# Convolution of batch 1 on 64-by-32 tiles with a shifted copy of x made by GpSimd and SyncE's queue

## The chip, the cores and the metric

The kernel runs on one core of a Trainium2 chip. Times are device microseconds. A time "before" or "after" is the median of its runs; the profile is one execution, taken by the hardware profiler. Engines are named TensorE (PE, with its weight loads PEld), VectorE (DVE), ScalarE (ACT), GpSimd (POOL) and SyncE (SP). The queues of GpSimd and SyncE issue most of the DMA transfers. A line such as L583 is a line of the kernel.

## The reference

For eight batches, x has 4224 rows of 192 features, in 8 heads of 24. A causal convolution with seven taps, whose weights are a softmax over the taps for each head, is followed by a mixer of rank 32 along the sequence and by a two-layer MLP with residual:

```
w    = softmax(weight, taps)                       # 8 heads x 7 taps
y[s] = sum_k w[head, k] * x[s - 6 + k]             # zero before the start
t    = y^T U                                       # 192 x 32, U is 4224 x 32
u    = y + (t V)^T                                 # V is 32 x 4224
out  = u + relu(u W1) W2                           # W1 192 x 768, W2 768 x 192
```

## The kernel before

**Tiles and groups.** A batch is 33 tiles of 128 rows; all 264 tiles form 33 groups of eight. The first MLP layer works on whole groups (`w1`, L554, into relu buffers `rl_sb`, of which there are three), the second on pairs of tiles (`w2`, L583; four pieces of 12 matmuls to a group), with the residual added on VectorE (L592) and the output sent on SyncE's queue (L600). PSUM has eight banks that are handed out in turn.

**The convolution.** x of a batch lies in `x_sb` as blocks of 64 rows: partitions 0 to 63 (r = 0) hold 32 blocks, partitions 64 to 127 (r = 1) the other 34. There are two `x_sb` buffers and one buffer `xb_sb`. Two forms exist:

- `conv` (L357 to L391) multiplies blocks with a banded matrix on 64-by-64 tiles of TensorE, the block itself and the block before it (halo) accumulated: eight matmuls a head.
- `conv32` (L317 to L353) uses 64-by-32 tiles. Each output strip of 32 rows then needs the 64 rows that end with it, so half of the strips read `x_sb` and half read `xb_sb`, a copy of x shifted by 32 rows. There too are eight matmuls a head, without accumulation.

`x_shift` (L277 to L315) makes `xb_sb` in six steps, all GpSimd copies: `same` for blocks 0 to 15 and for blocks 16 to 31 (L293, 128 partitions; with a small copy for the two extra blocks of r = 1, L295), and four `ahead` steps of 32 partitions (L305).

In the kernel before, batch 0 and batch 1 use `conv`, all others `conv32`.

**Start.** x of batch 0 is loaded in pieces (`KP`, `x_piece`): blocks for tiles 0 to 9 of both r, then the rest of r = 1, then the rest of r = 0. TensorE is kept busy by `idle` (L151 to L159) until the banded matrices are made by `band_half` (L234). The low-rank sum of batch 0 is taken in two ways: packed in four column strips for tiles that are ready early (`tt_mm`, 27 tiles), split in a high and a low part (`tt_split`) and added up by a matmul with `R4`; and as 128-wide matmuls on a fourfold copy of U (`tt_late`, 6 tiles). For groups 0 and 1, u is transposed by TensorE (`yT_part`, `hT_part`); for all later groups by a DMA transpose on SyncE's queue (`transp`, L498).

**The order of work.** `SLOTS` is written out by hand. A slot names groups for `w1`, groups for `w2`, and what is done ahead of which `w2` piece: `h3` makes u of group 3 (`h_group`) and issues its transpose, `t1` and `s1` are the packed sum and its adding up for batch 1, `c2:0:3:AAD` is a chunk of `conv32` (batch, first head, heads, engines that empty the banks), `d1` is the whole `conv` of batch 1 (with the transpose of group 3 held until its last matmul), `x2:6` issues all six steps of batch 2's shift, `l2:2` is the third load of x of batch 2, held until the last `w2` piece issued. Other loads of x are held until a given place in `w1` (`LOADS`), and the shift steps that are left are put between them.

**Queues.** Every engine and every queue works in program order. GpSimd issues all loads of x and of the weights and makes the shifted copies; SyncE issues the outputs and transposes.

Of the kernel before, what the change touches and what calls it, by code (L numbers as in the profile page):

```python
# [9 lines left out]
BF16 = mybir.dt.bfloat16  # L10
F32 = mybir.dt.float32
# [3 lines left out]
def kernel(  # L15
# [10 lines left out]
    nc = tc.nc  # L26
    P = nc.NUM_PARTITIONS
    B, S, D = x.shape
# [12 lines left out]
    QB = 32  # L41
# [14 lines left out]
    def bank():  # L56
        return psp.tile([P, 512], F32, name="ps", tag="ps")
# [18 lines left out]
    def x_part(b, r, s0, s1):  # L76

        blk = NB0 * r + s0 - 1
        return nc.gpsimd.dma_start(  # L79
            out=xt[b][HB * r : HB * r + HB, s0:s1, :],  # L80
            in_=x[b, blk * HB : (blk + s1 - s0) * HB, :].rearrange("(j p) d -> p j d", p=HB),
        )

    XP = [(0, 1, 17), (0, 17, NB0 + 1), (1, 0, 18), (1, 18, NB1 + 1)]

    KP = [{0: (0, 10), 1: (0, 10)}, {1: (10, NB1 // 2)}, {0: (10, NB0 // 2)}]

    def x_piece(k):
        for r, (k0, k1) in KP[k].items():
            x_part(0, r, (1 - r if k0 == 0 else 2 * k0 + 1), 2 * k1 + 1)  # L90

    def piece_tiles(k):
        return [NB0 // 2 * r + j for r, ks in KP[k].items() for j in range(*ks)]

    x_tile(0)
    x_piece(0)


    I32 = mybir.dt.int32
# [25 lines left out]
    )  # L125
    nlast = NT * 32 - nfull * P
    nc.gpsimd.dma_start(out=Ur[0:nlast, nfull, :], in_=U4[nfull * P :, :])
    for k in range(1, len(KP)):
        x_piece(k)


# [7 lines left out]
                in_=moe_w_ch1[:, m0:m1].rearrange("(c k) m -> k c m", k=HB),  # L139
            )  # L140

    zz = cst.tile([P, P], F32, name="zz")
    nc.vector.memzero(zz[:])

    rq = cst.tile([P, 2], F32, name="rq")
# [2 lines left out]
            nc.vector.memset(rq[QB * r : QB * r + QB, n : n + 1], v * r)  # L148
    wps = bank()

    def idle(n, w=4):  # L151
        for _ in range(n):
            nc.tensor.matmul(
                out=wps[:, 0 : w * P].rearrange("p (n t) -> p n t", t=P),
                lhsT=zz[:],
                rhs=zz[:].unsqueeze(1).to_broadcast([P, w, P]),
                start=True,
                stop=True,
            )  # L159

    idle(4)

# [112 lines left out]
            )  # L277

    band_half(0)
    idle(1, 2)  # L280
    band_half(1)


# [2 lines left out]
    def x_shift(b):  # L286
# [29 lines left out]
            ahead(1, m, NB1),  # L316
        ]  # L317

    steps = []

    def conv32(b, h0, nh, engs):
# [30 lines left out]
                    pp[part][:, 0 : nk[part] * GS].rearrange("p (k a) -> p k a", a=GS),  # L352
                )  # L353

    def conv(b, h0, nh, rs, engs, ks=((0, NB0 // 2), (0, NB1 // 2)), pp=None):

        if yt[b] is None:  # L357
            yt[b] = ys.tile([P, NT, D], BF16, name="y_sb")
        nk = {r: ks[r][1] - ks[r][0] for r in rs}
        if pp is None:  # L360
            pp = {r: bank() for r in rs}
        w = nh * GS
        for hh in range(nh):
            h = h0 + hh
            for halo in range(2):
                for r in rs:
                    for c in range(2):
                        st = 1 - halo + c + 2 * ks[r][0]
                        last = nc.tensor.matmul(  # L369
                            out=pp[r][HB * c : HB * c + HB, 0 : nk[r] * w].rearrange(  # L370
                                "p (k a) -> p k a", a=w
                            )[:, :, hh * GS : hh * GS + GS],
                            lhsT=bands[h // HQ][
                                HB * r : HB * r + HB, h % HQ, HB * halo : HB * halo + HB
                            ],
                            rhs=xt[b][
                                HB * r : HB * r + HB,
                                st : st + 2 * nk[r] - 1 : 2,
                                h * GS : h * GS + GS,
                            ],  # L380
                            start=(halo == 0),
                            stop=(halo == 1),
                            tile_position=(HB * r, HB * c),
                        )
        for n, r in enumerate(rs):
            j0 = NB0 // 2 * r + ks[r][0]
            evac(
                engs[n % len(engs)],
                yt[b][:, j0 : j0 + nk[r], h0 * GS : h0 * GS + w],
                pp[r][:, 0 : nk[r] * w].rearrange("p (k a) -> p k a", a=w),  # L390
            )  # L391
        return last
# [217 lines left out]
    def x_load(b, q, after):  # L610
        if q == 0:
# [5 lines left out]


    SLOTS = [
        ([0], [], {}),  # L620
        ([1], [0], {0: ["h0"], 1: ["h3", "l2:2"], 2: ["l2:3"]}),
        ([2], [1], {0: ["d1", "h1"], 1: ["t1"], 3: ["s1"], 4: ["h4", "x2:6"]}),
        ([3], [2], {1: ["h5"], 3: ["h6"]}),
        (
            [4, 5],
            [3, 4, 5],
            {
                0: ["h7"],
                2: ["c2:0:3:AAD"],
                3: ["c2:3:3:AAD"],  # L630
                4: ["c2:6:2:A", "x3:4"],
                6: ["t2"],
                8: ["s2"],
                9: ["h8"],
                11: ["h9"],
            },
        ),
    ]
    nh = 10
    for k in range(5, 14):  # L640
        gs = list(range(3 * k - 9, 3 * k - 6))
        hs = [f"h{g}" for g in range(nh, min(nh + 3, NG))] + [None] * 3
        nh = min(nh + 3, NG)
        if k == 5:
            at = {
                2: ["c3:0:3:AAD"],
                3: ["c3:3:3:AAD"],
                4: ["c3:6:2:A", "x4:3"],
                5: [hs[0]],
                6: ["t3"],  # L650
                8: ["s3", hs[1]],
                11: [hs[2]],
            }
        elif k < 10:
            b = k - 2
            at = {
                1: [f"c{b}:0:3:AAD"],
                2: [f"c{b}:3:3:AAD"],
                3: [f"c{b}:6:2:A"] + ([f"x{b + 1}:3"] if b + 1 < B else []),
                5: [f"t{b}", hs[0]],  # L660
                7: [f"s{b}"],
                8: [hs[1]],
                11: [hs[2]],
            }
        else:
            at = {0: [hs[0]], 4: [hs[1]], 8: [hs[2]]}
        SLOTS.append((gs, gs, {p: [w for w in what if w] for p, what in at.items()}))
# [5 lines left out]
        LOADS[b] = [(g, 0), (g, 3), (g + 1, 0), (g + 1, 3)]  # L673


    late = piece_tiles(2)
    U4_sb = cst.tile([P, len(late), 4, R], BF16, name="U4_sb")

    def tt_late(p):

        for n, j in enumerate(late):
            nc.tensor.matmul(
                out=p[:, 0:D],
                lhsT=U4_sb[:, n, :, :].rearrange("p a r -> p (a r)"),
                rhs=yt[0][:, j, :],
                start=False,
                stop=(n + 1 == len(late)),
            )

    for h in range(0, H, 2):  # L690
        conv(0, h, 2, [0, 1], "AA" if h == 0 else "AD", KP[0])
    work = [bank() for _ in range(4)]
    tp = bank()
    u_layout(work)
    x_tile(1)
    x_zero(1, nc.gpsimd)
    x_part(1, *XP[0])
    o = 0
    for r, (k0, k1) in KP[2].items():
        j = NB0 // 2 * r + k0  # L700
        nc.gpsimd.tensor_copy(
            out=U4_sb[:, o : o + k1 - k0, :, :],
            in_=U_sb[:]
            .rearrange("p k j r -> p (k j) r")[:, j : j + k1 - k0, :]
            .unsqueeze(2)
            .to_broadcast([P, k1 - k0, 4, R]),
        )
        o += k1 - k0

    NSL = (NT + 7) // 8 * 2  # L710
    V_sb = cst.tile([P, NSL, P], BF16, name="V_sb")
# [13 lines left out]
    W2_sb = cst.tile([P, MC, D], BF16, name="W2_sb")  # L725
    nc.gpsimd.dma_start(out=W2_sb[:], in_=moe_w_ch2[:].rearrange("(m p) d -> p m d", p=P))

    parts0 = [(0, 0, 2, bank(), "A"), (0, 2, 4, bank(), "D"), (1, 0, 4, bank(), "D")]
    yT_part(0, parts0)
    def conv_piece(k):  # L730
        for n, h in enumerate(range(0, H, 3)):
            for r in KP[k]:
                conv(0, h, min(3, H - h), [r], "AD"[n % 2], KP[k], {r: work[n]})

    conv_piece(1)
    tt_mm(0, piece_tiles(0) + piece_tiles(1), tp)
    tt_split(0, tp)
    conv_piece(2)
    ps0 = work[3]
    for n, part in enumerate(ttb[0]):  # L740
        nc.tensor.matmul(out=ps0[:, 0:D], lhsT=R4[:], rhs=part[:], start=(n == 0), stop=False)
    more = [(2, 0, 2, bank(), "A"), (2, 2, 4, bank(), "A")]
    yT_part(0, more[0:1])
    tt_late(ps0)
    yT_part(0, more[1:])
    parts1 = [(0, 0, 4, bank(), "A")]
    yT_part(1, parts1)
    tt_done(0, ps0)
    hT_part(0, parts0 + more)
    rest = [(c, 0, 4, bank(), "ADA"[c]) for c in (1, 2)]  # L750
    yT_part(1, rest)
    hT_part(1, parts1 + rest)
    band2 = cst.tile([P, H, QB], BF16, name="band2")
    for xp in XP[1:]:
        x_part(1, *xp)
# [8 lines left out]
    def do(what):  # L764
        if what[0] == "c":
            b, h0, n, engs = what[1:].split(":")
            conv32(int(b), int(h0), int(n), engs)
            return
        if what[0] == "d":
            for h in range(H):  # L770
                last = conv(int(what[1:]), h, 1, [0, 1], "AA" if h == 2 else "AD")
            held(transp(3), last)
            return
        if what[0] == "l":
            b, q = (int(v) for v in what[1:].split(":"))
# [8 lines left out]
        n = int(what[1:])  # L784
        if what[0] == "h":
            h_group(n)
            if n > 1 and n != 3:
                transp(n)
        elif what[0] == "t":
            tt_split(n, tt_mm(n, range(NT)))  # L790
        else:
            tt_sum(n)
# [55 lines left out]
```

## Time and profile before

| What | Value |
|---|---|
| median of three runs | 325.29 us (325.09 to 325.36) |
| profiled execution | 325.29 us, of which the span of the core is 323.5 |
| busy share of the span | TensorE 98%, weight loads 69%, VectorE 83%, ScalarE 53%, GpSimd 44% |
| one GpSimd copy to `xb_sb`, 128x3072 | 2.74 us |
| one GpSimd copy to `xb_sb`, 32x3072 | 2.74 us |
| output of 192 KB, median from issue to landing | 2.7 us |
| load of x of 384 or 432 KB, median | 7.3 us |
| DMA transpose, median | 3.9 us |

A page of the profile gives each engine's busy time and groups of instructions. A row of the timeline is: start, length, engine, line, operation, output and input, count, and in brackets the idle time ahead of it with what ended it. A row of the chain is: start, length, engine, tile, line. Busy time of TensorE includes waits inside its pipeline, so what it does with its time is read from the order of its work in the chain.

### The profile page before, as it was taken

What the parts mean: (1) busy time and instruction counts of PE and PEld (TensorE: products, weight loads), DVE (VectorE), ACT (ScalarE), POOL (GpSimd) and SP (SyncE); (2) the same over time, 40 slices, a digit from 0 to 9 for tenths busy, and PEclk for the clock granted to TensorE, in tenths of its full rate; (3) what the DMA queues carried; (4) which work ended last, traced back from release to release, by engine and by line L of the source; (5) the groups of instructions that cost most, each with busy time, mean ns of one, the idle gap of its engine ahead of it and who ended that gap; (6) DMA issues with size and microseconds to landing.
All of it is one profiled execution on the core that took longest, in us unless ns stands there. A gap on an engine that the chain in (4) does not pass through costs nothing.

```text
span 323.5 us, 9584 instructions
## 1 busy us (share of the span) xinstructions
PE 317.1 (98%) x3996; PEld 223.2 (69%) x3996; DVE 269.1 (83%) x551; ACT 170.4 (53%) x344; POOL 142.7 (44%) x111
## 2 busy tenths in 40 slices
PE   6999999999999999999999999999999999999996
PEld 3757676478677647866864784587797497487495
DVE  6769989987977986998798699879898897896864
ACT  1766624860874397088339708824903902912920
POOL 8664179729947694786859497000000000000000
PEclk9999999999999999999999999999999999999999
DMA  8999993999996899699699976139269059048035
GB/s 104 192 192 178 209 211 99 203 195 248 210 153 180 229 175 169 170 162 195 166 238 183 192 162 181 33 112 244 58 168 267 8 149 268 25 121 271 2 119 176
DMA packets 122907, 53.52 MB, mean 165 GB/s; under 512 B 87760, under 2 KB 122832, under 8 KB 122864
## 3 DMA queue, kind: packets, MB, share of 16 engines
q1 hardware_dynamic: 84528, 38.08, 47.0%
q0 software_dynamic: 38192, 14.73, 39.6%
q8 instruction: 31, 0.51, 0.7%
q14 instruction: 12, 0.10, 0.1%
q10 hardware_dynamic: 144, 0.10, 0.1%
HBM read 29.49 MB, written 25.95 MB: 171 GB/s over the span
## 4 chain that ended last, share of the span: by engine, by line
PE 92%; ACT 3%; DMA 2%; DVE 1%; issue 0%; POOL 0%; POOLq 0%
PE ps L583 42%; PE ps L554 39%; PE ps L339 3%; PE ps L457 3%; DMA x_sb<-in_x_dram 2%; PE ps L402 2%; ACT rl_sb L568 2%; PE ps L369 1%; ACT y_sb L256 1%; PE ps L509 1%; DVE u_sb L479 1%; DVE rl_sb L570 1%; PE ps L524 0%; PE ps L428 0%; POOL x_sb L79 0%
## 5 line engine op out<-in xcount | busy, mean ns | idle before, releaser
L568 ACT ACTIVATE rl_sb<-ps 128x512 bf16<-128x512 f32 x233 | 124.3, 603 | 108.0 <-PE ps L554 96.0
L583 PE MATMUL ps<-W_sb,rl_sb 128*128 128x192 bf16 x1584 | 141.9, 246 | 0.2
L583 PEld LDWEIGHTS <-rl_sb 128*128 128x128 bf16 x1584 | 128.1, 98 | 13.5 <-issue 13.1
L554 PE MATMUL ps<-uT,W_sb 64*128 64x512 bf16 x1188 | 131.7, 376 | 0.0
L570 DVE TENSOR_SCALAR rl_sb<-ps 128x512 bf16<-128x512 f32 x163 | 105.3, 688 | 15.7 <-PE ps L554 15.4
L554 PEld LDWEIGHTS <-W_sb 64*128 64x128 bf16 x1188 | 66.9, 94 | 60.5 <-issue 3.9
L592 DVE TENSOR_TENSOR out_sb<-ps,u_sb 128x384 f32<-128x384 f32 (+1 forms) x133 | 70.4, 550 | 25.9 <-PE ps L583 25.4
L305 POOL COPY xb_sb<-x_sb 32x3072 bf16<-32x3072 bf16 (+1 forms) x24 | 67.6, 2826 | 0.7
L479 DVE TENSOR_TENSOR u_sb<-y_sb,ps 128x192 bf16<-128x192 bf16 (+1 forms) x168 | 66.3, 461 | 0.0
L293 POOL COPY xb_sb<-x_sb 128x3072 bf16<-128x3072 bf16 x12 | 32.6, 2744 | 34.6 <-PE ps L339 25.7
L256 ACT ACTIVATE y_sb<-ps 128x384 bf16<-128x384 f32 (+4 forms) x90 | 38.2, 514 | 10.7 <-PE ps L339 7.9
L79 POOL DMA_DIRECT2D x_sb<-in_x_dram x32 | 27.1, 849 | 17.5 <-PE ps L554 10.5
L258 DVE CAST y_sb<-ps 128x408 bf16<-128x408 f32 (+4 forms) x36 | 19.2, 578 | 1.1 <-PE ps L369 0.9
L457 PE MATMUL ps<-tt_sb,V_sb 32*128 32x192 bf16 x264 | 12.4, 246 | 0.1
L339 PE MATMUL ps<-xb_sb,band 64*32 64x384 bf16 x192 | 12.1, 332 | 0.0
L339 PE MATMUL ps<-x_sb,band 64*32 64x384 bf16 x192 | 12.1, 333 | 0.0
L457 PEld LDWEIGHTS <-V_sb 32*128 32x128 bf16 x264 | 4.7, 92 | 7.3 <-issue 7.3
L416 ACT ACTIVATE tt_hi<-ps 128x192 bf16<-128x192 f32 x8 | 2.6, 331 | 10.9 <-PE ps L402 10.9
L369 PE MATMUL ps<-x_sb,band 64*64 64x240 bf16 (+3 forms) x192 | 8.1, 276 | 0.3 <-DMA x_sb<-in_x_dram 0.3
L369 PEld LDWEIGHTS <-band 64*64 64x64 bf16 x192 | 6.0, 106 | 2.2 <-issue 1.5
L339 PEld LDWEIGHTS <-band 64*32 64x32 bf16 x384 | 4.5, 89 | 4.1 <-issue 3.0
L402 PE MATMUL ps<-y_sb,U_sb 128*32 128x192 bf16 x258 | 7.4, 247 | 0.0
(65 smaller groups left out, 69.0 us busy)
## 6 DMA issues: line engine op xcount, KB each, us to landing
out_dram<-out_sb SPq DMA_DIRECT2D x131, 192.0 KB, 2.7
x_sb<-in_x_dram POOLq DMA_DIRECT2D x14, 384.0 KB, 7.3
x_sb<-in_x_dram POOLq DMA_DIRECT2D x7, 432.0 KB, 7.3
x_sb<-in_x_dram POOLq DMA_DIRECT2D x7, 408.0 KB, 8.0
x_sb<-in_x_dram POOLq DMA_DIRECT2D x1, 504.0 KB, 7.6
uT<-u_sb SPq DMA_TRANSPOSE x31, 3.9
x_sb<-in_x_dram POOLq DMA_DIRECT2D x1, 480.0 KB, 5.9
W_sb<-in_moe_w_ch_dram POOLq DMA_DIRECT2D x2, 192.0 KB, 7.6
```

The source lines that it names most:

```text
L79: return nc.gpsimd.dma_start(out=xt[b][HB * r : HB * r + HB, s0:s1, :], in_=x[b, blk * HB : (blk + s1 - s0) * HB, :].rearrange("(j p) d -> ...
L256: nc.scalar.activation(out=out, in_=in_, func=ACT.Copy)
L293: nc.gpsimd.tensor_copy(out=xbt[b][:, s0:s1, :], in_=xt[b][:, s0 + 1 : s1 + 1, :])
L305: nc.gpsimd.tensor_copy(out=xbt[b][q, s0:s1, :], in_=xt[b][q, s0:s1, :])
L339: nc.tensor.matmul(out=pp[r][QB * cg : QB * cg + QB, 0 : nk[r] * GS], lhsT=w[hr], rhs=t[hr, st : st + 2 * nk[r] - 1 : 2, hs], start=True, ...
L457: nc.tensor.matmul(out=banks[pr][:, a * D : (a + 1) * D], lhsT=V_sb[32 * q : 32 * q + 32, (j // 8) * 2 + j % 2, :], rhs=ttb[b][32 * q : 32 ...
L479: nc.vector.tensor_tensor(out=u_group(g)[:, i : i + n, :, hf, :], in0=yt[b][:, run[0] : run[0] + n, :].rearrange("p n (c k) -> p n c k", c=3),
L554: last = nc.tensor.matmul(out=pps[m][hf][:], lhsT=W1_sb[HB * hf : HB * hf + HB, c, m * P : (m + 1) * P], rhs=uTt[g][HB * hf : HB * hf + HB ...
L568: nc.scalar.activation(out=rl[:, m, hf, :], in_=pp[hf][:], func=ACT.Relu)
L570: nc.vector.tensor_scalar_max(out=rl[:, m, hf, :], in0=pp[hf][:], scalar1=0.0)
L583: last = nc.tensor.matmul(out=cps[:, a * D : (a + 1) * D], lhsT=rlt[g][:, m, hf, (i + a) * P : (i + a + 1) * P], rhs=W2_sb[:, m, :], start ...
L592: nc.vector.tensor_tensor(out=o[:, 0:n, :].rearrange("p n (c k) -> p n c k", c=3), in0=cps[:, 0 : n * D].rearrange("p (n c k) -> p n c k", ...
```

## The change

1. Batch 1 goes through `conv32` too, in three chunks of three, three and two heads, put ahead of the third, fourth and fifth place among the `w2` pieces of slot 2. Its `xb_sb` is made by GpSimd's two `same` steps (`X1`, issued in slot 0, so ahead of the loads of batch 2 on GpSimd) and by four copies inside SBUF on SyncE's queue (`x_ahead`): two (`w0`) in slot 0, two (`w1`) in slot 2 ahead of its first `w2` piece. The transpose of group 3 is no longer held. Note that in a slot's list `w1` names this step, not the MLP layer.
2. W2 of group 3 moves from slot 4 to slot 3; the sum of batch 1 and the making of groups 4 to 9 move with it; `c2` and `c3` start with two heads in place of three. The third and fourth load of batch 2 move from slot 1 to slot 2.
3. At the start, the pieces of x are four in place of three (the same four transfers), the packed sum has 20 tiles in place of 27, and `tt_late` 13 in place of 6. The transposes of groups 0 and 1 are in a simpler order. `idle` takes five and one full matmuls in place of four full and one half.

```diff
-    KP = [{0: (0, 10), 1: (0, 10)}, {1: (10, NB1 // 2)}, {0: (10, NB0 // 2)}]
+    KP = [(0, 0, 10), (1, 0, 10), (1, 10, NB1 // 2), (0, 10, NB0 // 2)]
...
-    idle(4)
+    idle(5)
...
-    idle(1, 2)
+    idle(1)
...
+    def x_ahead(b, n):
+
+        for r in range(2):
+            q = slice(HB * r + QB, HB * r + HB)
+            s0, s1 = ((0, NB0 // 2), (NB0 // 2, (NB0, NB1)[r]))[n]
+            nc.sync.dma_start(out=xbt[b][q, s0:s1, :], in_=xt[b][q, s0:s1, :])
...
-        ([0], [], {}),
-        ([1], [0], {0: ["h0"], 1: ["h3", "l2:2"], 2: ["l2:3"]}),
-        ([2], [1], {0: ["d1", "h1"], 1: ["t1"], 3: ["s1"], 4: ["h4", "x2:6"]}),
-        ([3], [2], {1: ["h5"], 3: ["h6"]}),
+        ([0], [], {0: ["X1", "w0"]}),
+        ([1], [0], {0: ["h0"], 1: ["h3"]}),
+        (
+            [2],
+            [1],
+            {
+                0: ["w1", "h1"],
+                1: ["l2:2"],
+                2: ["c1:0:3:AAD"],
+                3: ["c1:3:3:AAD", "l2:3"],
+                4: ["c1:6:2:AD", "x2:6"],
+            },
+        ),
+        ([3], [2, 3], {0: ["t1"], 1: ["s1"], 2: ["h4"], 4: ["h5"], 6: ["h6"]}),
         (
             [4, 5],
-            [3, 4, 5],
+            [4, 5],
             {
                 0: ["h7"],
-                2: ["c2:0:3:AAD"],
-                3: ["c2:3:3:AAD"],
-                4: ["c2:6:2:A", "x3:4"],
+                2: ["c2:0:2:A"],
+                3: ["c2:2:3:AAD"],
+                4: ["c2:5:3:AAD", "x3:4"],
                 6: ["t2"],
-                8: ["s2"],
-                9: ["h8"],
-                11: ["h9"],
+                7: ["s2"],
+                8: ["h8"],
             },
         ),
...
+        if what == "X1":
+            for step in x_shift(1)[0:2]:
+                step()
+            return
+        if what[0] == "w":
+            x_ahead(1, int(what[1:]))
+            return
...
-            if n > 1 and n != 3:
+            if n > 1:
                 transp(n)
```

## The prediction

> **What bounds the kernel now.** I read first the page's engine shares and the chain that ended last:
>
> ```profile
> PE 317.1 (98%) x3996; PEld 223.2 (69%) x3996; DVE 269.1 (83%) x551; ACT 170.4 (53%) x344; POOL 142.7 (44%) x111
> PE 92%; ACT 3%; DMA 2%; DVE 1%; issue 0%; POOL 0%; POOLq 0%
> ```
>
> TensorE sets the end, so what counts is the time it loses or saves in its own order of work. Next the chain in order of time, around the convolution of batch 1 and, for comparison, that of batch 3, which already runs on 64-by-32 tiles:
>
> ```profile
> 33.92 2.09 PE ps L554 x18
> 36.02 2.54 ACT rl_sb L568 x5
> 38.56 3.10 ACT y_sb L256 x8
> 41.70 1.15 PE ps L583 x12
> ...
> 95.16 0.64 PE ps L339 x19
> 95.80 1.10 PE ps L583 x12
> 96.89 0.71 PE ps L339 x17
> 97.60 1.10 PE ps L583 x12
> 98.70 0.47 PE ps L339 x11
> 99.17 1.10 PE ps L583 x12
> ```
>
> In the timeline batch 1's matmuls start at 37.84 (64 of them, L369) and W2 resumes at 41.70: 3.86 us, of which h1's eight matmuls are some 0.35, leaves 3.5 for the convolution. Batch 3's takes 0.64+0.71+0.47 = 1.82 in three chunks between W2 pieces.
>
> Then the two queues that the change loads, GpSimd's and SyncE's, in the timeline:
>
> ```profile
> 21.24 1.73 POOL L79 DMA_DIRECT2D x_sb<-in_x_dram  x2 [1.22 <-DMA x_sb<-in_x_dram]
> 22.96 2.28 POOL L759 COPY band<-band 32x128 bf16<-32x128 bf16 x8
> 29.38 2.48 POOL L79 DMA_DIRECT2D x_sb<-in_x_dram  x3 [3.91 <-PE ps L457]
> 42.52 5.43 POOL L293 COPY xb_sb<-x_sb 128x3072 bf16<-128x3072 bf16 x2 [8.89 <-DMA x_sb<-in_x_dram]
> ```
> ```profile
> 32.16 3.76 SPq L600 DMA_DIRECT2D out_dram<-out_sb  x4
> 41.13 1.53 SPq L498 DMA_TRANSPOSE uT<-u_sb  x1
> ```
>
> GpSimd has time from 25 to 42, but two copies of 128x3072 take 5.43 there. Last, transfers by tile and window. First the two loads of x of batch 1 issued between 22 and 23; then two outputs issued at 34.9 and 35.4, beside loads of batch 2; then one at 46.4, beside none:
>
> ```profile
> DMA to landing us min/median/max: 7.3/8.2/9.1
> ```
> ```profile
> L600 SPq DMA_DIRECT2D out_dram<-out_sb x2: 429/464/498, 34.9 to 35.4; - x2
> DMA to landing us min/median/max: 7.0/7.4/7.8
> ```
> ```profile
> L600 SPq DMA_DIRECT2D out_dram<-out_sb x1: 372/372/372, 46.4 to 46.4; - x1
> DMA to landing us min/median/max: 2.7/2.7/2.7
> ```
>
> A 192 KB transfer of SyncE's queue lands in 2.7 us alone and in 7 to 8 beside loads of x. The outputs of 69.7 to 70.9, beside batch 3's loads, took 6.3 to 6.5.
>
> [...]
>
> **The change, part by part.**
>
> *Start.* One more idle matmul (4 to 5) and the second idle made twice as wide. The first eight passes took 5.15 us and ended at 6.22; a warm pass is some 0.43 (from the weight loads at 4.34, 4.77 and 5.20), so two more, and the clearing of zz that is some 0.3 longer, end at 7.4. The band matmuls wait for DVE's pr until 7.60 anyway. The wider idle matmul moves the second band from 8.78 to about 8.95, and the convolution waits for x until 9.89. Hidden; if that cover went, at most 0.6. I take +0.1 with the next item.
>
> *Low-rank sum of batch 0.* Seven tiles leave the packed sum (27 matmuls, 14.60 to 15.49) for the late one (0.095 each at L682: 6 in 0.57): +0.67 -0.23 in matmul time. But the packed sum no longer waits for r = 1's last evacuation (its second part began at 15.15), which gives about 0.4 back. The transposes are only reordered. Net 0. GpSimd's second U4 copy (0.8 us at 13.6) ends before it waits for W_sb at 17.72.
>
> *Convolution of batch 1 by conv32.* -3.5 +1.82 = -1.7; counting from slot 2's whole length (33.92 to 47.28) it is -1.45. I take -1.5. DVE has one evacuation less.
>
> *Moved steps.* The sums t1, s1 and h4 move to slot 3, W2 of group 3 into slot 3, h9 into slot 5: the same TensorE work. DVE in slot 3 then has 5 relus at 0.69, 8 outputs at 0.55, three h at 2.06 and 0.7 for the sums: 14.7 us against some 14.2 of TensorE. Slot 4 is lighter by one group. I take +0.3, less the 0.2 that DVE catches up in the stall below. uT of group 4 is ready about 1 us ahead of its W1; uT of group 3 is no longer held until after the convolution.
>
> *GpSimd's part of the shift, X1.* It needs x of batch 1. The third load was issued at 21.24 and took 7.3, so landed at 28.5; the fourth, at 22.1 with 9.1, at 31.2. The copies of 2.74 run 28.5-31.3 and 31.3-34.05, the halo copy of 0.5 ends at 34.55. Queued behind them on GpSimd are the loads of batch 2: the first two move from 29.4 to 34.75 and 35.6, in flight until about 42. Its last two are also moved, to 39.3 and after the first chunk. Batch 2's shift (17.2 us) then ends near 65 to 67, and its convolution comes near 70 to 72 instead of 66.95: covered by 3 to 5 us. For batches 3 and 4 this cover is 0.3 to 1.
>
> *SyncE's part, w0 and w1.* w0's two copies wait for GpSimd until 31.3, when no load is in flight: landed near 34; behind them the first output (32.16) loses nothing. w1's two copies stand behind group 0's outputs and behind transpose 3, which is no longer held: DVE's h3 adds end at 33.99, the transpose holds the queue 1.5, three outputs 0.4 each, so the copies are issued at 36.8 and 37.2, in the middle of batch 2's loads. Behind them are only group 1's outputs, with eight buffers.
>
> When does TensorE want them? W1 of group 2 ends at 37.84 as now; h1 0.35, two W2 pieces 1.1 each: first chunk at 40.45. Lower bound for the landing: an output alone, 2.1 (at 47.6) gives 39.3, no wait. Upper bound: transpose at 67.4, beside loads, 8.3 gives 45.5. I take 6.8, among the 6.2 to 7.8 of outputs beside batch 2's loads, since those loads are again in flight and three outputs and a transpose stand ahead: 44.0. TensorE works in order, so it waits 44.0 - 40.45 = 3.5 us, and W2 pieces queued behind wait too.
>
> *Sum.* 325.29 (the profiled execution: span 323.5 and 1.79 around it; it is also the median) +0.1 -1.5 +0.1 +3.5 = 327.5.
>
> **Rivals.**
> 1. *The copies are in time.* [...] Then 325.3 -1.5 +0.4 = 324.2. It decides from a landing before about 41.55, which leaves a wait of 1.1; under 4.4 us after issue. Against it: no output beside loads landed in under 5.3.
> 2. *Longer wait and clock drop.* The last two loads join at 39.3, and transpose 3 with three outputs goes first: landing at 46, wait 5.5[...]: 329.5 to 331.
> 3. *GpSimd becomes the bound.* With the copies in time, batch 2's loads and shifts come 4 to 5 us later, so the shifts of batches 3 and 4 end with their convolutions (before, batch 4's shift ended 121.7, its chunk began 122.40): the gain is eaten, 325.0 to 325.8.
> 4. *The change does little:* a wait of about 1, 325.3.
>
> **How the numbers follow.** A difference under 0.2% (0.65 us) can't be told from none. Forecast (wait 2 to 5) 0.62, its own range 326.0 to 329.0; rival 1 0.16; rivals 3 and 4 0.09, a third of it over the bound; rival 2 0.13. Slower 0.62+0.13+0.03 = 0.78, same 0.06, faster 0.16. The range runs from rival 1's 324.3 to 330.0, taking in most of rival 2.
>
> **What would show it.** Right: TensorE idle of about 3.5 us ahead of L342's first matmuls on batch 1, near 40.5, ended by a DMA into xb_sb; the copies at L320 of w1 issued near 37 with 6 us or more to landing, w0's with about 3; GpSimd's copies at L289 at 28.5 and 31.3; the slots after slot 3 as long as before. Wrong: that idle under 1 us, w1's copies landing within 4 us, or new idle in front of batch 3's or 4's convolution.

## The result and the profile after

| What | Before | After |
|---|---|---|
| median | 325.24 us (325.09 to 325.69) | 339.22 us (336.31 to 340.70) |
| ratio | 1 | 1.042, 95% interval 1.037 to 1.047 |
| profiled execution | 325.29, span 323.5 | 340.70, span 338.9 |

The change makes the kernel 14 us slower; the forecast was 2.2 us slower, with 330.0 as the upper end of the range. Here and below, times are medians of all executions, and ratios are of means without the slow executions, of which e5 had one and k3 two. First the two lines of the page of the changed kernel that answer to those shown of before, engine shares and the chain that ended last:

```profile
PE 321.9 (95%) x3998; PEld 223.2 (66%) x3998; DVE 269.4 (79%) x550; ACT 171.1 (50%) x345; POOL 149.7 (44%) x115
PE 72%; POOL 10%; DMA 9%; DVE 5%; issue 2%; ACT 1%; POOLq 0%; DVEq 0%
```

TensorE held 92% of the chain before; now 19% lies with GpSimd and with transfers. Its waits by engine and line from 20 us on, changed kernel (before has none there):

```profile
PE ps L342 <- DMA xb_sb<-x_sb: 6.1, 1, 6.1
PE ps L342 <- POOL xb_sb L301: 3.2, 1, 3.2
```

**The first loss** is in front of the first chunk of batch 1. TensorE's timeline there:

```profile
37.94 2.15 PE L586 MATMUL ps<-W_sb,rl_sb 128*128 128x192 bf16 x24
...
46.21 0.48 PE L342 MATMUL ps<-xb_sb,band 64*32 64x384 bf16 x1 [6.11 <-DMA xb_sb<-x_sb]
...
48.01 2.10 PE L586 MATMUL ps<-W_sb,rl_sb 128*128 128x192 bf16 x12
```

A W2 piece of 12 matmuls takes 2.10 us at 48, where two of them took 2.15 at 38. The table by stretches says why (columns: stretch, its length, busy time and count of PE, PEld, DVE, ACT, POOL, then the granted clock of TensorE, the DMA share and GB/s):

```profile
40.00:42.00 2.00, 0.10 (x2) 0.00 (x0) 1.28 (x3) 0.00 (x0) 0.25 (x1) 1.00 1.42 190
42.00:44.00 2.00, 0.00 (x0) 0.00 (x0) 0.00 (x0) 0.00 (x0) 0.00 (x0) 0.63 1.32 253
...
50.00:52.00 2.00, 2.00 (x31) 1.11 (x31) 1.58 (x3) 1.36 (x4) 0.89 (x1) 0.50 0.22 67
52.00:54.00 2.00, 2.00 (x31) 1.24 (x30) 0.89 (x3) 0.87 (x3) 0.30 (x1) 0.81 0.85 100
```

The clock falls to one half at 42.5, 2.4 us after the idle time begins, and comes back only near 52.8, more than 6 us after TensorE resumed. The two queues, SyncE's and GpSimd's, in the timeline of the changed kernel:

```profile
31.47 1.23 SPq L320 DMA_DIRECT2D xb_sb<-x_sb  x2
32.76 0.58 SPq L603 DMA_DIRECT2D out_dram<-out_sb  x1
33.84 1.61 SPq L501 DMA_TRANSPOSE uT<-u_sb  x1
35.49 1.69 SPq L603 DMA_DIRECT2D out_dram<-out_sb  x3
37.28 1.57 SPq L320 DMA_DIRECT2D xb_sb<-x_sb  x2
```
```profile
28.70 5.49 POOL L289 COPY xb_sb<-x_sb 128x3072 bf16<-128x3072 bf16 x2 [3.27 <-DMA x_sb<-in_x_dram]
...
34.93 1.63 POOL L79 DMA_DIRECT2D x_sb<-in_x_dram  x2
39.41 0.85 POOL L79 DMA_DIRECT2D x_sb<-in_x_dram  x1 [2.85 <-PE ps L586]
50.91 0.89 POOL L79 DMA_DIRECT2D x_sb<-in_x_dram  x1 [10.66 <-PE ps L342]
```

w0's copies land in 3.0 us, w1's, beside loads of batch 2, in 8.6 and 8.7 (the answer for that tile and stretch):

```profile
L320 SPq DMA_DIRECT2D xb_sb<-x_sb x2: 732/739/746, 37.3 to 38.1; - x2
...
DMA to landing us min/median/max: 8.6/8.7/8.7
```

Slot 4 starts at 68.3; with the moved slots of part 2 alone it starts at 60.4 (e3 below). So 7.9 us are lost by then: 6.1 of idle time and some 2.9 of half clock (e2), less 1.5 for the cheaper convolution; about 0.4 is left for small differences.

**The second loss** is in slots 5 and 6, which take 29.8 and 33.3 us instead of 28.3 and 28.0 (slot 5 starts 7.1 us later than before, slot 7 13.8). The chain in order of time shows what sets it:

```profile
75.90 10.09 DMA x_sb<-in_x_dram
...
86.10 2.74 POOL xb_sb L289
...
103.39 13.79 DMA x_sb<-in_x_dram
...
117.23 2.75 POOL xb_sb L289
...
131.58 3.09 POOL xb_sb L301
...
134.71 1.22 PE ps L342 x18
```

For nearly 60 us the chain runs through loads of x and GpSimd's shifts, and TensorE waits 3.2 us for the last step of batch 4's shift, again with half clock behind it (from 134.7 to 138.1). The load at 103.39 lands in 13.8 us; before, the same load, issued at 91.4, landed in 8.0. From slot 7 to slot 13 both kernels take the same time. The last 1.6 us of the 15.4 in the span come after the last output is issued: from there to the end of the span it is 4.4 us, 2.8 before, and that output itself lands in 2.7 us, 1.7 before.

### The profile page after: what moved, and what is told of

Its sections match the earlier page's. It is cut to its first block, busy times and chain, and to the rows that moved or that the text cites. A ratio compares the mean times of both kernels' runs of the same rounds, so it can differ in the third digit from the quotient of the medians.

```text
span 338.9 us, 9609 instructions
## 1 busy us (share of the span) xinstructions
PE 321.9 (95%) x3998; PEld 223.2 (66%) x3998; DVE 269.4 (79%) x550; ACT 171.1 (50%) x345; POOL 149.7 (44%) x115
## 3 DMA queue, kind: packets, MB, share of 16 engines
q1 hardware_dynamic: 84720, 38.90, 45.8%
## 4 chain that ended last, share of the span: by engine, by line
PE 72%; POOL 10%; DMA 9%; DVE 5%; issue 2%; ACT 1%; POOLq 0%; DVEq 0%
PE ps L586 33%; PE ps L557 30%; DMA x_sb<-in_x_dram 7%; POOL xb_sb L301 6%; PE ps L342 3%; PE ps L460 2%; POOL x_sb L79 2%; DMA out_dram<-out_sb 2%; POOL xb_sb L289 2%; DVE u_sb L482 1%; PE ps L405 1%; PE ps L372 1%; ACT rl_sb L571 1%; DVE pr L208 1%; PE ps L512 1%
## 5 line engine op out<-in xcount | busy, mean ns | idle before, releaser
L586 PE MATMUL ps<-W_sb,rl_sb 128*128 128x192 bf16 x1584 | 144.5, 249 | 0.1
L586 PEld LDWEIGHTS <-rl_sb 128*128 128x128 bf16 x1584 | 130.1, 99 | 14.7 <-issue 14.1
L557 PEld LDWEIGHTS <-W_sb 64*128 64x128 bf16 x1188 | 65.1, 94 | 62.3 <-issue 4.4
L289 POOL COPY xb_sb<-x_sb 128x3072 bf16<-128x3072 bf16 x14 | 38.2, 2744 | 36.3 <-DMA x_sb<-in_x_dram 19.1
L252 ACT ACTIVATE y_sb<-ps 128x408 bf16<-128x408 f32 (+4 forms) x91 | 38.6, 509 | 27.4 <-PE ps L342 24.9
L342 PE MATMUL ps<-xb_sb,band 64*32 64x384 bf16 (+1 forms) x224 | 16.4, 363 | 9.5 <-DMA xb_sb<-x_sb 6.1
L342 PEld LDWEIGHTS <-band 64*32 64x32 bf16 x448 | 5.6, 93 | 15.3 <-issue 13.7
L342 PE MATMUL ps<-x_sb,band 64*32 64x384 bf16 x224 | 15.5, 365 | 0.0
L155 PE MATMUL ps<-zz 128*128 128x512 f32 x12 | 7.3, 759 | 1.5 <-DVE zz L145 1.5
L419 ACT ACTIVATE tt_hi<-ps 128x192 bf16<-128x192 f32 x8 | 2.7, 332 | 10.6 <-PE ps L405 10.5
L420 DVE TENSOR_TENSOR tt_lo<-ps,tt_hi 128x192 bf16<-128x192 f32 x8 | 2.9, 356 | 4.3 <-ACT tt_hi L419 4.3
```

The source lines that it names most:

```text
L252: nc.scalar.activation(out=out, in_=in_, func=ACT.Copy)
L289: nc.gpsimd.tensor_copy(out=xbt[b][:, s0:s1, :], in_=xt[b][:, s0 + 1 : s1 + 1, :])
L342: nc.tensor.matmul(out=pp[r][QB * cg : QB * cg + QB, 0 : nk[r] * GS], lhsT=w[hr], rhs=t[hr, st : st + 2 * nk[r] - 1 : 2, hs], start=True, ...
L557: last = nc.tensor.matmul(out=pps[m][hf][:], lhsT=W1_sb[HB * hf : HB * hf + HB, c, m * P : (m + 1) * P], rhs=uTt[g][HB * hf : HB * hf + HB ...
L586: last = nc.tensor.matmul(out=cps[:, a * D : (a + 1) * D], lhsT=rlt[g][:, m, hf, (i + a) * P : (i + a + 1) * P], rhs=W2_sb[:, m, :], start ...
```

## The experiments

All ratios are to the kernel before, measured beside the runs in question; its medians lay between 325.16 and 325.39. Theories were given letters in the order in which they came up; D to G are spelled out in the texts of the runs. "Lands in" is the time from issue to landing.

### The wait for w1

**e1_w1_early**: w1's copies in slot 0, behind w0's.

```diff
-        ([0], [], {0: ["X1", "w0"]}),
+        ([0], [], {0: ["X1", "w0", "w1"]}),
-                0: ["w1", "h1"],
+                0: ["h1"],
```

> The two late copies into xb_sb are issued right behind the two early ones, ahead of the first output and of the loads of batch 2. Theory A (two separate losses: the copies beside the loads cost 6.5 us of wait and 2.5 us of half clock; GpSimd's shorter time between the convolutions costs some 5 us in slot 6): the copies land within 3 to 4 us, near 38, the wait ahead of batch 1's first chunk is gone, slot 6 stays long, 330 us. Theory B (the late shifts and loads of batches 3 and 4 only follow from the first wait): both go, 324 to 325.5 us. Theory C (the 64-by-32 form itself costs more than it saves): over 334 us.

Measured: 340.08 us, ratio 1.043 (1.040 to 1.047). The copies are issued at 34.0 and 34.5, land in 2.9 and 3.2, and the wait in front of batch 1 is gone; W1 of group 2 to the end of the third chunk takes 10.55 us against some 12.0 for the same work before, so the 1.5 of the cheaper convolution is there. (The 12.0 is slot 2's 13.4 us without the sum of batch 1 and h4, which the changed kernel does later.) But SyncE's queue stood still until GpSimd's second copy was done, so transpose 3, behind the copies, is issued at 35.8 instead of 33.8: now beside the loads of batch 2. It lands in 12.8 us instead of 3.5. The waits of e1:

```profile
PE ps L557 <- DMA uT<-u_sb: 9.0, 2, 4.7
PE ps L342 <- POOL xb_sb L301: 4.0, 2, 2.4
```

The wait taken away came back as waits for transposes and for GpSimd.

**e2_kept_warm**: seven idle matmuls of 512 columns, results unused, ahead of the first chunk of batch 1, so that TensorE works while it waits.

```diff
-                2: ["c1:0:3:AAD"],
+                2: ["f7", "c1:0:3:AAD"],
```

> The changed kernel with seven idle float32 matmuls into a bank of their own ahead of batch 1's first chunk, where TensorE waits; they take 6 us at full clock. If the half clock after the wait costs what its slices show, 2.5 us go: 336.5 us, and the clock stays at 1.0 from 40 to 56. If the loss is the wait alone: 339 us.

Measured: 337.68 us, ratio 1.038 (1.036 to 1.041). The clock stays at full speed there. Slot 4 starts at 65.9 instead of 68.3, 2.4 us sooner, although the first chunk starts 0.5 us later (46.7 instead of 46.2): from that chunk to slot 3 the same work takes 4.4 us instead of 7.3, so the half clock behind the wait is worth some 2.9 us there. Over the whole kernel the medians differ by 1.5.

### Part 2 of the change, and one transpose

**e3_w2_moved_alone**: the kernel before with W2 of group 3 in slot 3 and the lists of slots 4 and 5 of the changed kernel. The sum of batch 1, h4 and the loads of batch 2 stay where they were, so this is part 2 without what it moves out of slots 1 and 2.

```diff
-        ([3], [2], {1: ["h5"], 3: ["h6"]}),
+        ([3], [2, 3], {4: ["h5"], 6: ["h6"]}),
...
-            [3, 4, 5],
+            [4, 5],
...
```

> The kernel before with W2 of group 3 moved into slot 3, groups 5 to 9 and the chunks of batches 2 and 3 placed as in the changed kernel, convolution of batch 1 as before. Theory A (the move alone leaves GpSimd 4 us less between batch 2's convolution and slot 5): waits ahead of batch 3's or 4's convolution, 326.5 to 330 us. Theory B: within 0.5 us of before, 325.2 us.

Measured: 329.89 us, ratio 1.013 (1.010 to 1.016). By the ratio this part costs 4.3 us alone, where the prediction had +0.1. The wait and the transpose ahead of it, in e3's waits and in SyncE's timeline:

```profile
PE ps L339 <- POOL xb_sb L305: 2.0, 1, 2.0
```
```profile
95.10 1.52 SPq L498 DMA_TRANSPOSE uT<-u_sb  x1
```

The row at 95.10 is the transpose of group 9, moved with h9 from the end of slot 4 to the head of slot 5. It lands in 8.7 us, and batch 4's last load, issued at 95.3, lands in 12.7 (before: 8.0). GpSimd gets it at 108.05 and is late for batch 4's convolution. The wait of 2.0 us also has half clock behind it, from 126.6 to 130.0, which is some 1.7 us of lost work (half of 3.4; an estimate from this trace): wait and clock together account for 3.7 of the 4.3 us.

**f3_w2_moved_h9_back**: e3 with h9 back at the end of slot 4, and slot 5's order of before.

```diff
-                8: ["h8"],
+                8: ["h8", "h9"],
...
-                0: [hs[0]],
...
-                6: [hs[1]],
-                7: ["t3"],
-                9: ["s3", hs[2]],
-                11: ["h12"],
+                5: [hs[0]],
+                6: ["t3"],
+                8: ["s3", hs[1]],
+                11: [hs[2]],
```

> e3_w2_moved_alone (329.9) with one difference: the sum h9 and its transpose are back at the end of slot 4 and slot 5 has the order of before, so that no transpose is issued beside the first loads of batch 4. Theory D: the loads of batch 4 land in 6 to 8 us, the wait of 2.0 us for GpSimd in front of batch 4's convolution is gone, 325.2 to 327 us. Rival (the four W2 tiles taken out of slot 4 leave GpSimd too short a time for the shift of batch 3 and 4): 329 us or more, with the same wait for GpSimd.

Measured: 326.30 us, ratio 1.003 (1.000 to 1.005). The wait for GpSimd and the half clock are gone, and by the ratios 3.4 of the 4.3 us with them. The order of slot 5 went back together with h9, so the two are not told apart. The loads of batch 4 are not as short as expected (5.9 and 10.8 us for the last two), and about 1 us stays.

**g3_after_h9_back**: the changed kernel with that difference, h9 and slot 5's order.

> The changed kernel with one difference: the sum h9 and its transpose are back at the end of slot 4, and slot 5 has the order of before. If the second loss of the changed kernel (5 to 6 us in slots 5 and 6) comes from the transposes beside batch 4's loads, as f3 against e3 suggests (3.6 us): 333 to 335.7 us, and TensorE's wait of 3.2 us for GpSimd in front of batch 4's convolution is gone. If it comes from the late end of batch 2's shift, handed on by GpSimd: 338 us or more.

Measured: 336.54 us, ratio 1.034 (1.030 to 1.037): 2.7 us under the changed kernel and 0.8 over what the text gives for the transposes, so between the two expectations. The wait for GpSimd in front of batch 4 has shrunk to 2.1 us and is not gone. h9's place is one part of the second loss, not all of it.

**f1_before_unheld**: the kernel before with transpose 3 issued right behind h3.

```diff
-            held(transp(3), last)
...
-            if n > 1 and n != 3:
+            if n > 1:
```

> The kernel before with one difference: the transpose of group 3 is issued right behind its sum h3, as in the changed kernel, and no longer waits for the last matmul of batch 1's convolution. Theory D (a DMA transpose in flight beside loads of x stretches both): it is issued at about 31 us, lands in 10 to 13 us, the loads of batch 2 (29.4 to 32.7) take 12 to 20 us instead of 5.9 to 12.2, and the kernel is slower, 328 to 335 us. Rival (the held transpose was only a matter of order, the transfers don't mind each other): 325.2 within 0.5 us, the transpose in 5 us.

Measured: 325.73 us, ratio 1.002 (0.999 to 1.006). The transfers mind each other as theory D says: the transpose, issued at 33.9, lands in 11.9 us and the last load in 13.4 instead of 12.2. The cost does not follow: u of group 3 is there at 45.8, before W1 of group 3 starts at 47.1. A stretched transfer costs nothing as long as nobody waits for it; D as a forecast of time falls.

**f4_start_alone**: the kernel before with part 3 of the change alone, and before's slots.

> The kernel before with the start of the changed kernel alone (x of batch 0 in four pieces, low-rank sums in two late parts, the wider idle matmuls), and with before's slots from the first W1 layer on. The prediction put this part at +0.1 us: 325.3 us, between 324.9 and 325.7. If the start hands later slots a worse order of transfers it is slower, 326 or more.

Measured: 325.88 us, ratio 1.001 (0.999 to 1.003). The start costs 0.6 us between the medians and nothing that the interval tells from zero.

### Batch 1's shift, in the slots of before

**e5_early_w2_kept**: changed kernel with w1 early, batch 1's chunks at the first two places of slot 2, and the later slots of before. **f2_early_held**: the same with transpose 3 held. By its code the hold is the last matmul of the third chunk, which is the last of batch 1's convolution; the expectation has the second chunk's.

> The changed kernel with the late copies issued early as in the first run, batch 1's chunks ahead of the first and second W2 piece of slot 2, and slots 3 to 5 as in the kernel before (W2 of group 3 not moved). Theories A and B: no wait ahead of batch 1 and GpSimd's time as before, so only the gain of the 64-by-32 form is left: 323.6 to 324.6 us. Theory C: 325.2 us or more.

> e5_early_w2_kept with one difference: the transpose of group 3 is issued after the second chunk of batch 1's convolution and held behind its last matmul. Theory D: the loads of batch 2 land in 6 to 13 us again, the waits of 11.2 and 4.6 us in front of batch 2's convolution and of a slot are gone, 323.3 to 325.5 us. Rival (GpSimd's order, not the transfers, made e5 slow): 335 us or more.

Measured: e5 345.81 us, ratio 1.060 (1.055 to 1.064); f2 337.30, ratio 1.037 (1.034 to 1.040). Neither part 2 nor w1's place is in these any more, and they are as slow as the changed kernel or slower. f2 waits 7.7 us for transpose 3, which is issued at 42.6 and lands in 12.2 us, because the loads of batch 2 are still in flight: the last, issued at 37.2, lands in 18.2. Holding moved the collision, and D fell here too. With the chunks packed into two places the cheaper convolution gave only 0.1 us (slot 2 from 33.84 to some 47.1, against 33.85 to 47.22 before). Both kernels share GpSimd's copies in slot 0, which led to the next runs.

**g2_before_shift_alone**: the kernel before, with GpSimd's two copies of batch 1 in slot 0; nothing reads them. **g1_before_shift_copies**: with the four copies of SyncE's queue as well, also unread.

```diff
-        ([0], [], {}),
+        ([0], [], {0: ["X1"]}),
```

> As g1, without the four copies on SyncE's queue: GpSimd's two copies alone, unused. Theory E, with the order on GpSimd as the cause: 330 to 339 us, nearly as much as g1. Rival (the copies inside SBUF, 0.77 MB on the transfer engines, are the cause): 325.3 to 327 us, 5 us or more under g1. The prediction's cover of 3 to 5 us for batch 2's shift would give 325.3 to 326 here.

```diff
-        ([0], [], {}),
+        ([0], [], {0: ["X1", "w0", "w1"]}),
```

> The kernel before with batch 1's two shift copies on GpSimd and the four copies on SyncE's queue (w0 and w1) put into slot 0; nothing reads what they write, and the convolution of batch 1 stays as before. Theory E (GpSimd's two copies stand ahead of the loads of batch 2, which start 5.3 us later and then meet transpose 3 and the outputs of group 1): the loads are issued at 34.8 to 37.2 and the last lands at 50 us or later, TensorE waits in front of batch 2's convolution, and the kernel takes 333 to 339 us, as e1, e5 and f2 did (337 to 346). Rival (the 64-by-32 convolution and its place in slot 2 made these slow): 325 to 327 us.

Measured: g2 331.34 us, ratio 1.019 (1.018 to 1.021); g1 336.51, ratio 1.036 (1.030 to 1.042). Two copies that nobody reads, on an engine that is idle more than half of the time, cost 6.1 us. GpSimd's timeline in g2, and transpose 3 in the answer for its tile:

```profile
28.65 5.46 POOL L293 COPY xb_sb<-x_sb 128x3072 bf16<-128x3072 bf16 x2 [3.48 <-DMA x_sb<-in_x_dram]
...
34.85 3.36 POOL L79 DMA_DIRECT2D x_sb<-in_x_dram  x4
```
```profile
L498 SPq DMA_TRANSPOSE uT<-u_sb x1: 2683/2683/2683, 41.5 to 41.5; - x1
...
  PE ps L554: 4.2, 1
...
DMA to landing us min/median/max: 10.3/10.3/10.3
```

The loads start 5.5 us later than before, the last lands at 51.6 instead of 44.9, and transpose 3 meets them: 10.3 us instead of 5.2, a wait of 4.2 us, and half clock from 52.3 to 55.7. g1 adds 0.8 MB of copies: the last load lands at 55.8, the transpose in 12.2, and TensorE waits 6.1.

**m1_shift_behind_loads**: g2 with the two copies behind the loads of batch 2.

```diff
-        ([0], [], {0: ["X1"]}),
+        ([0], [], {}),
-        ([1], [0], {0: ["h0"], 1: ["h3", "l2:2"], 2: ["l2:3"]}),
+        ([1], [0], {0: ["h0"], 1: ["h3", "l2:2"], 2: ["l2:3", "X1"]}),
```

> g2_before_shift_alone (331.3) with one difference: GpSimd's two copies of batch 1, still unused, stand behind the four loads of batch 2 instead of ahead of them. Theory G (the place ahead of the loads is the cause, not the work of the copies: late loads meet transpose 3 or hand their delay to GpSimd's shifts): the loads are issued at 29.4 to 32.7 again, the copies run in GpSimd's idle time from 33.6 to 39.1, 325.0 to 325.6 us. Rival [...]: 327 us or more.

```profile
29.36 2.48 POOL L79 DMA_DIRECT2D x_sb<-in_x_dram  x3 [3.78 <-PE ps L457]
32.72 0.89 POOL L79 DMA_DIRECT2D x_sb<-in_x_dram  x1 [0.88 <-PE ps L583]
33.65 5.43 POOL L293 COPY xb_sb<-x_sb 128x3072 bf16<-128x3072 bf16 x2
```

Measured: 325.37 us, ratio 1.000 (0.997 to 1.003). The same copies, the same work: 6.1 us or nothing, by their place in GpSimd's queue; the copies themselves cost the other engines nothing that the interval tells from zero.

**k2_shift_alone_unheld**: g2 with transpose 3 not held, as in the changed kernel.

> g2_before_shift_alone (331.3) with one difference: the transpose of group 3 is not held behind batch 1's convolution; it is issued when h3's sums are done, at about 33.9 us, before the first late load of batch 2 (34.8). Theory F (the two copies cost time only because they move batch 2's loads onto transpose 3, which is held until 41.5, lands in 10.3 us and keeps TensorE waiting 4.2 us at W1 of group 3): the transpose lands by 40 us, that wait is gone, 325.2 to 326.5 us. Rival (the late loads of batch 2 reach TensorE by GpSimd's shifts as well): 328 us or more, with a wait for GpSimd or a DMA in front of a convolution.

Measured: 338.36 us, ratio 1.040 (1.039 to 1.042), 7 us over g2. Theory F fell. Transpose 3 lands in 3.2 us and slots 2 and 3 are on time, as F says, but the delay then reaches TensorE by GpSimd. k2's waits and GpSimd's timeline:

```profile
PE ps L339 <- POOL xb_sb L305: 10.6, 3, 7.4
```
```profile
57.08 11.25 POOL L305 COPY xb_sb<-x_sb 32x3072 bf16<-32x3072 bf16 x4
...
68.51 3.37 POOL L79 DMA_DIRECT2D x_sb<-in_x_dram  x4
85.93 2.74 POOL L293 COPY xb_sb<-x_sb 128x3072 bf16<-128x3072 bf16 x1 [14.05 <-PE ps L554]
```

Batch 2's shift ends at 68.3 (before: 59.8), batch 3's loads are all issued behind it at 68.5 to 71.0 (before: 60.0 to 64.3), beside a row of outputs, and land in 7.7 to 18.8 us. The delay grows from step to step: 5.4 us at batch 2's first load, 8.5 at the end of its shift, and TensorE waits up to 7.4 us in front of a convolution. In g2 the wait at transpose 3 had given GpSimd that time: slot 4 starts at 62.4 there, 6.1 us later than in k2, and TensorE waits for GpSimd nowhere.

### Attempts to put the transfers in order

**g4_shift_half_on_scalar**: f2 with the second half of batch 1's shift on ScalarE, which is idle there, and w1 in slot 1.

> f2_early_held (337.3) with the second half of batch 1's shift on ScalarE, idle from 30.3 to 34.8, and w1 behind it. GpSimd then holds the loads of batch 2 only until 31.4. Theory E: the loads start 3.3 us sooner than in f2, the last lands near 48 instead of 55.4, and most of f2's loss is gone: 325 to 330 us, with a wait of some us for w1's copies, which now fly beside the loads. Rival (the start of the loads is not what counts): 335 us or more.

Measured: 334.20 us, ratio 1.031 (1.026 to 1.037). ScalarE's copy takes 2.76 us at 31.6; the loads start at 31.5, and the waits for transposes are gone. But w1's copies, issued at 35.4 and 36.3 beside the loads, land in 7.8 and 7.7, TensorE waits 4.8 us for them, and half clock follows (from 40.8 to 47.6). So it ends between the two expectations, a net 3.1 us under f2: the loads start sooner, and w1 pays for it.

**k4_before_conv_in_order**: the kernel before with batch 1 on 64-by-32 tiles, and transpose 3, w1's copies and the loads of batch 2 one behind another.

```diff
-        ([0], [], {}),
-        ([1], [0], {0: ["h0"], 1: ["h3", "l2:2"], 2: ["l2:3"]}),
+        ([0], [], {0: ["X1", "w0"]}),
+        ([1], [0], {0: ["h0"], 1: ["h3", "w1"]}),
...
-    LOADS = {2: [(1, 5), (1, 5)], 3: [(4, 1), (4, 4), (5, 1), (5, 4)]}
+    LOADS = {2: [(2, 1), (2, 2), (2, 3), (2, 4)], 3: [(4, 1), (4, 4), (5, 1), (5, 4)]}
...
```

**k3_after_in_order**: g3 with the same two moves.

> The kernel before with batch 1 convolved in 64-by-32 tiles, GpSimd's and SyncE's shift in slot 0 and slot 1, and the three users of the transfer engines put one behind another: transpose 3 right behind h3, then w1's copies, and the loads of batch 2 held behind blocks 1 to 4 of W1 of group 2, so issued at about 36.5 to 39.5 us. Theory F: transpose 3 lands by 38 and w1 by 40 us, no wait in front of batch 1's chunks, and the 1.5 us of the cheaper convolution are kept: 323.5 to 325 us. Rival (GpSimd's shifts of batches 2 and 3 then end too late, since the loads come 7 us later than before): 326 us or more, with a wait for GpSimd in front of batch 2's or 3's convolution.

> g3_after_h9_back (336.5) with w1's copies right behind transpose 3 and the loads of batch 2 held behind blocks 1 to 4 of W1 of group 2, as in k4. Theory F: the wait of 6.4 us and the half clock behind it are gone, and of the 15 us that the changed kernel lost at most 2 are left: 324.5 to 327 us. Rival (the slots of the change lose time of their own): 329 us or more.

Measured: k4 334.92 us, ratio 1.028 (1.026 to 1.031); k3 337.25, ratio 1.035 (1.033 to 1.037). In k4 transpose 3 lands in 3.3 us, but the second of w1's two copies, issued at 36.0, still meets the first loads (35.6) and lands in 6.2: a wait of 2.8 us with half clock. Later, outputs beside batch 3's loads land in 11 us and TensorE waits 2.7 us for VectorE's output step, again with half clock; that the output buffers ran out is the likely reason. k3's only trace is of an execution of 347.03 us, 10 us above its median, and doesn't stand for it; in it the wait for w1 is down to 1.8 us, but TensorE waits 6.6 us for GpSimd and 5.8 for a transpose. No order that was tried gets the three users of the transfer engines through in time.

**m2_after_shift_behind_loads**: g3 with GpSimd's copies behind the loads of batch 2, and these at the places of before.

> g3_after_h9_back (336.5) with GpSimd's two copies of batch 1 behind the loads of batch 2, and these at the places that they had before (29.4 to 32.7); w0's copies follow, w1's stay in slot 2. Theory G: GpSimd's shifts of batches 2 to 4 are on time again, the later waits for GpSimd are gone, but batch 1's chunk still waits 5 to 8 us for w1's copies with the half clock behind it: 331.5 to 334.5 us. Rival (what is left over in g3 beside the wait for w1 has nothing to do with GpSimd's order): 336 us or more.

```profile
PE ps L342 <- DMA xb_sb<-x_sb: 9.5, 1, 9.5
PE ps L342 <- POOL xb_sb L301: 0.9, 1, 0.9
```

Measured: 339.53 us, ratio 1.042 (1.038 to 1.047), not faster. The wait for GpSimd in front of batch 4 falls from 2.1 to 0.9 us, as theory G says of GpSimd's part; but w1's copies are issued at 39.5 and 40.2 and land in 9.7 us, so the wait in front of batch 1 grows from 6.4 to 9.5. Slots 5 and 6 together take 58.5 us instead of g3's 59.5 (56.4 before). The run moves more than it was meant to: w0's copies, which were alone in g3 (2.9 and 3.0 us), now follow GpSimd's at 37.0 and land in 9.3 and 9.6. What the loads win, the copies lose.

## Why the prediction was wrong

- **Start, low-rank sum of batch 0 (+0.1): right.** f4 gives 0.6 at most, not told from zero.
- **Convolution of batch 1 (-1.5): right as a price.** e1 shows 1.5 where its operands are there and the chunks have three places. One reading behind it was off: h1's matmuls took 0.63 us there and not 0.35 (41.02 to 41.65), so the old convolution took 3.2 us and not 3.5.
- **w0 and GpSimd's copies: right.** 28.7, and landings of 3.0 us, where about 3 was forecast.
- **w1's copies (+3.5): right in kind, too small, and the largest miss that is measured in the changed kernel itself.** They were issued at 37.3 and 38.1 (forecast 36.8 and 37.2) and landed in 8.7 us where 6.8 was taken from outputs beside loads; the upper bound of 8.3 was too low as well. The wait is 6.1. The clock was put only into rival 2, where its share of the 329.5 to 331 was an estimate of the author's that no trace of before shows; it is some 2.9 in e2, and the sum had nothing for it. Rival 1, the copies in time, needed a landing under 4.4 us, and no trace showed one beside loads. Rival 2's wait, with that clock, was the better account of this place: about 7.9 us net at slot 4 and not 2.2.
- **Moved steps (+0.1): wrong, a failed step.** "the same TensorE work" is true, and the 4.3 us of e3 come from elsewhere: 3.4 of them go when h9 and slot 5's order go back (f3); in the changed kernel it is 2.7 (g3). The prediction counted VectorE's work of the moved steps and left out that h9 takes a DMA with it, onto SyncE's queue beside batch 4's loads.
- **GpSimd's part, X1 (nothing): wrong, the failed step with the largest cost when it is tried alone.** The prediction saw the loads of batch 2 move to 34.75 and 35.6, as they did. It called batch 2 "covered by 3 to 5 us", gave batches 3 and 4 "0.3 to 1", and still charged nothing. Its landing times for the late loads were those of the early ones ("in flight until about 42"; they landed at 43.4 and 48.7). g2, m1 and k2 show in its place: the order alone costs 6.1 us if transpose 3 is held and 13.1 if it is not, and nothing behind the loads. That is in the kernel before. What X1's place costs inside the changed kernel is not shown: with the copies behind the loads (m2) slots 5 and 6 got 1.0 us shorter, and w1's copies landed late all the same. Rival 3 had this mechanism, priced at the gain that it would eat.
- **"the slots after slot 3 as long as before": wrong.** Slots 5 and 6 are 6.7 us longer. The sign named for it, idle time in front of batch 4's convolution, is there.

By place, the profiled execution is 7.1 us late at the start of slot 5, where 2.2 were forecast, loses 6.7 in slots 5 and 6, and 1.6 after the last output is issued, where nothing was. g3 can be set against f3, which has the same slots 4 and 5 without the convolution's change and the new start: g3 is 6.8 us later at the starts of slots 4 and 5, 9.0 at slot 7 and 10.6 at the end. So some 2.2 us in slots 5 and 6 are due neither to h9 nor to the wait for w1 itself. A late GpSimd is the likely reason, since TensorE still waits 2.1 us for it there; of these 2.2 us m2 took back 1.0.

The costs of the parts do not add up to the whole: g1's 11.3 and e3's 4.3 already come to more than 14. As g2 against k2 shows, a wait in one place gives GpSimd time in another. The 1.6 us at the end stay open: the kernels whose convolution of batch 1 reads SyncE's copies end 4.1 to 4.4 us after the last output's issue (3.8 in k3's trace), g1 (copies unread) 3.4, f1 (no copies at all) 3.7, and the others 2.7 to 2.8. Nor did any run beat the kernel before.

## What to carry to other kernels

An engine that is mostly idle is not free: if it issues loads in program order, a copy put ahead of them delays every later load (in g2 two copies, 5.46 us together, made the loads start 5.5 us later and cost 6.1), and the cover to count is that of the whole chain of load, shift and next load, not that of the first link. When a step is moved, list its transfers and what else is in flight at the new place; a transfer priced beside other traffic needs the longest landing seen there (w1's copies took 8.7 us where 6.8 was charged), and the others grow too (in f1 the last load from 12.2 to 13.4). And a wait of TensorE is to be charged with half clock behind it: in these traces every wait of 3.2 us or more brought it, and some from 1.9 us on did; each 3.4 us at half clock takes up to 1.7 from a busy TensorE (an estimate: the half of it; e2 showed 2.9 for 6.5 us of work at half clock).

## What the runs showed of the hardware that was not expected

- **A DMA transpose beside loads of x** landed in 8.7 to 12.8 us in the runs above (e3, g2, f1, f2, g1, e1), against 3.2 to 3.5 with little in flight (k2, k4, the changed kernel).
- **Copies inside SBUF** of 192 KB on SyncE's queue took 2.9 to 3.2 us alone (the changed kernel, g3, e1) and 6.2 to 9.7 beside loads of x (k4 and m2 the ends); they came off no better than outputs to DRAM of the same size, which took 2.7 alone and 7.0 and 7.8 beside loads in the kernel before. Loads issued beside a row of outputs took up to 18.8 us in k2, where the median of its loads of 384 KB is 8.3.
- **Half clock came in whole steps of 3.4 us.** In the traces of these runs (k3's left aside) sixteen stretches at half clock lie behind a wait of TensorE: six of 3.4 us, six of 6.8, three of 10.2 and one of 13.7, all multiples of 3.41. They begin 2.1 to 5.0 us after the idle time began, in e2, e3, g2 and the first one of e1 only when TensorE was already at work again. The length of a wait alone didn't decide: waits of 1.9 us (e2), 2.0 (e3), 2.7 and 2.8 (k4) brought half clock, waits of 2.1 (g3), 2.4 (e1) and 2.9 (e5) did not, and all of 3.2 or more did.
- **Copies on GpSimd, no loss to the other engines.** GpSimd's two unread copies of 128x3072 beside VectorE's work cost nothing where they delayed no load (m1: ratio 1.000).
